# A list scheduler orders the first phase of a gated scan and feed-forward kernel; low parts and clips change engines

## The chip, the cores and the metric

The kernel runs on one core of one Trainium2 chip. The metric is device time in microseconds (us) of one execution. Engines are named as in the profile: PE is TensorE's matmul, PEld its weight load, DVE is VectorE, ACT is ScalarE, POOL is GpSimd, SP is SyncE, whose queue issues the DMA transfers here.

## The reference

Two parts follow each other. A gated recurrence over 6080 positions of 2 sequences with 256 channels, and a feed-forward layer on all 12160 tokens (256 to 2048 to 256), in float32:

```
sig = 1 / (1 + exp(-f_logit));  f = lb + (1 - lb) * sig;  i = 1 - f
h[t] = f[t] * h[t-1] + i[t] * x[t]            # per channel
a = h @ w_in                                  # 256 -> 2048
g = a where a >= 1;  0 where a <= -1;  (a + 1)**2 / 4 between
y = g @ w_out                                 # 2048 -> 256
```

The weights are float64 in memory: they arrive as pairs of 32-bit words and are turned into floats on the chip.

## The kernel before

**Tiles and numbers.** Channels lie on the 128 partitions (two halves k), tokens along the free dimension. The tokens are cut into tiles of 384, 512, 512, 512, and then 512 each. Every number that TensorE multiplies is split into a high part (a cast to fp32r) and a low part (value minus high part), and each product is three matmuls: high by high, low weight by high, high by low. A *unit* (t, u) is tile t by 256 of the 2048 hidden channels, with two halves j. For each j there are six matmuls into a PSUM bank (`mm_h`, L294 to L303; *H block* here), then the activation, then six matmuls that add to the tile's two output banks (`mm_o`, L347; *O block*). "H20" below is the two H blocks of unit (2, 0).

**The activation** of one half: `clip` to -1..1 from the PSUM bank (DVE, L310), (c/2 + 1/2)**2 (ACT, L313), maximum with the bank (`top`, DVE, L318), which frees the bank, the cast to the high part (ACT, L325), the subtraction for the low part (`g_lo`, POOL, L332).

**The weights.** There are 17 jobs (two of half size), each a load of 512 KB, whose words are taken apart: `conv1a` masks the exponent (DVE, L149), shifts it (ACT, L150) and masks the fraction (DVE, L151); `conv1b` joins fraction and lower word (DVE, L160) and scales (ACT, L163); `conv2` adds the sign (DVE, L172), multiplies (DVE, L179 or L184), casts the high part (ACT, L185) and subtracts the low part (POOL, L186).

**The recurrence** of one tile and half: `gate` (ACT, L228), `inp` (DVE, L250), `forget` (ACT, L241), `scan` (DVE, L267), high part (ACT, L274), low part (POOL, L279).

**The phases.** The *first phase* takes tiles 0 to 2 through all eight u (24 units in eight *rounds* of three, u from 0 to 7) while the weights are converted. Its PE order in the loop is H block, O block of two units earlier, H block, O block; six of eight PSUM banks hold the outputs of three tiles, so that two are left for H blocks. Tile 3 follows alone (the loop at L788), then pairs of tiles in a plan of fixed times. In all phases the order of an engine's instructions is the order in which the program emits them. In the first phase this order is written out by hand: rounds from u = 1 run in the loop of L493, with one step of a list `fill` (a half of a conversion, or a step of tile 3's recurrence) behind each clip:

```
for j in JA:
    mm_h(t, u, [j])
    if j == 0 and i > T0:
        g_lo(*units[i - 1], nc.gpsimd)
    clip(t, u, j)
    step = fill.pop(0) if fill else None
    ...
    top(t, u, j)
    if i > T0:
        mm_o(*units[i - LAG], [j])
```

Of the kernel before, what the change touches and what calls it, by code (L numbers as in the profile page):

```python
# [7 lines left out]
F32 = mybir.dt.float32  # L8
BF16 = mybir.dt.bfloat16
F32R = mybir.dt.float32r  # L10
I32 = mybir.dt.int32
# [10 lines left out]
def token_tiles(total):  # L22

    out, s = [], 0
    while s < total:
        n = SIZES[len(out)] if len(out) < len(SIZES) else NMAX
        assert s + n <= total
        out.append((s, n))
        s += n
    return out  # L30


@with_exitstack
def gated_scan_then_ffn_kernel(
# [58 lines left out]
    mol = const.tile([P, KD], F32, name="mol")  # L93
    half = const.tile([P, 1], F32, name="half")
# [47 lines left out]
    def conv1a(j):  # L142
        r = raw[j]
        hi = r[..., 1]
        ea = sp.tile([P, 2, *hi.shape[1:]], I32, tag="s", name="ea")
        e, a = ea[:, 0], ea[:, 1]
        exps[j], mants[j] = e, a

        nc.vector.tensor_single_scalar(out=flat(e), in_=flat2(hi), scalar=0x7FF00000, op=ALU.bitwise_and)  # L149
        nc.scalar.activation(out=flat(e), in_=flat(e), func=AF.Relu, bias=ebias, scale=8.0)  # L150
        nc.vector.tensor_single_scalar(out=flat(a), in_=flat2(hi), scalar=0x000FFFFF, op=ALU.bitwise_and)  # L151

    flat2 = flat3 = flat

    def conv1b(j):

        lo = raw[j][..., 0].bitcast(U32)
        v = sp.tile(list(lo.shape), F32, tag="s", name="v")
        vals[j] = v
        nc.vector.scalar_tensor_tensor(  # L160
            out=flat(v), in0=flat(lo), scalar=2.0**-32, in1=flat(mants.pop(j)), op0=ALU.mult, op1=ALU.add
        )
        nc.scalar.activation(out=flat(v), in_=flat(v), func=AF.Identity, bias=one, scale=2.0**-20)  # L163

    def conv1(j):
        conv1a(j)
        conv1b(j)

    def conv2(j, eng):
        e, v = exps.pop(j), vals.pop(j)  # L170
        _, hi, lo = jobs[j]
        nc.vector.scalar_tensor_tensor(  # L172
            out=flat(e), in0=flat(raw.pop(j)[..., 1]), scalar=-0x80000000, in1=flat(e),
            op0=ALU.bitwise_and, op1=ALU.bitwise_or,
        )
        if len(v.shape) == 4:

            for k in range(KD):
                nc.vector.scalar_tensor_tensor(  # L179
                    out=flat3(v[:, k]), in0=flat3(v[:, k]), scalar=oml[:, k : k + 1],  # L180
                    in1=flat3(e[:, k].bitcast(F32)), op0=ALU.mult, op1=ALU.mult,
                )
        else:
            nc.vector.tensor_tensor(out=flat(v), in0=flat(v), in1=flat(e.bitcast(F32)), op=ALU.mult)  # L184
        nc.scalar.copy(out=hi, in_=v)  # L185
        eng.tensor_tensor(out=lo, in0=v, in1=hi, op=ALU.subtract)  # L186
# [107 lines left out]
    def mm_h(t, u, js=JA):  # L294
        n = tiles[t][1]
        for j in js:
            ops = []
            for w, x in ((wi_hi, xhi), (wi_lo, xhi), (wi_hi, xlo)):
                ops += [(w[:, u, k, j], x[t, k][:, :n]) for k in range(KD)]
            for i, (a, b) in enumerate(ops):  # L300
                nc.tensor.matmul(  # L301
                    out=acc[t, u][j][:, :n], lhsT=a, rhs=b, start=(i == 0), stop=(i == len(ops) - 1)
                )  # L303

    def clip(t, u, j):
        n = tiles[t][1]
        if (t, u) not in gg:
            gg[t, u] = gp.tile([P, 2, NMAX], F32, tag="g", name="g")
        c = gg[t, u][:, j, :n]
        nc.vector.tensor_scalar(  # L310
            out=c, in0=acc[t, u][j][:, :n], scalar1=-1.0, scalar2=1.0, op0=ALU.max, op1=ALU.min
        )
        nc.scalar.activation(out=c, in_=c, func=AF.Square, bias=half, scale=0.5)  # L313

    def top(t, u, j):
        n = tiles[t][1]
        c = gg[t, u][:, j, :n]
        nc.vector.tensor_tensor(out=c, in0=c, in1=acc[t, u][j][:, :n], op=ALU.max)  # L318

    def g_hi(t, u, js=JA):  # L320
        n = tiles[t][1]
        if js[0] == 0:
# [4 lines left out]
    def g_lo(t, u, eng, js=JA):  # L327
        n = tiles[t][1]
        if js[0] == 0:
# [43 lines left out]
    with tc.manual_schedule():  # L373
# [8 lines left out]
        load_x(0, K0, (fv, fin, "f"))  # L382
        nc.sync.dma_start(out=lb, in_=lower_bound.rearrange("(k p) -> p k", p=P))
        load_w(0)
        load_x(0, K0, (xv, xin, "x"))
        load_x(0, K1)
        load_w(1)
        load_x(1, KA)
        load_w(2)
        load_x(2, KA)  # L390
        nc.vector.tensor_scalar(
            out=oml, in0=lb, scalar1=-1.0, scalar2=1.0, op0=ALU.mult, op1=ALU.add
        )
# [12 lines left out]
        gate(1, K0)
        forget(1, K0, nc.scalar, True)
        inp(0, K1)
        scan(0, 1)
        x_hi(0, K1)  # L410
        x_lo(0, K1, nc.gpsimd)
        conv1(1)
        conv2(1, nc.gpsimd)
        gate(1, K1)
        forget(1, K1, nc.scalar, True)
        inp(1, K0)
        scan(1, 0)
        x_hi(1, K0)
        x_lo(1, K0, nc.gpsimd)
        gate(2, KA)  # L420
        inp(1, K1)
        scan(1, 1)
        x_hi(1, K1)
        x_lo(1, K1, nc.gpsimd)
# [4 lines left out]
        units += [(t, u) for t in range(T0, NC) for u in range(NU)]  # L429

        for t in range(3):
            acc[t, 0] = [bank(), bank()]
        mm_h(0, 0)
        clip(0, 0, 0)
        mm_h(1, 0)
        conv1a(2)
        for k in (K0, K1):
            inp(2, k)
            forget(2, k, nc.scalar)
        for k in (K0, K1):  # L440
            scan(2, k.start)
            x_hi(2, k)
            x_lo(2, k, nc.gpsimd)
        clip(0, 0, 1)
        conv1b(2)
        mm_h(2, 0)
        conv2(2, nc.gpsimd)
        for j in JA:
            top(0, 0, j)
            g_hi(0, 0, [j])  # L450
            g_lo(0, 0, nc.gpsimd, [j])
        for j in JA:
            clip(1, 0, j)
        keep_warm(6, po[0, 0])
        load_w(3)
        load_w(4)
        conv1a(3)
        conv1b(3)
        for j in JA:
            top(1, 0, j)  # L460
            g_hi(1, 0, [j])
            g_lo(1, 0, nc.gpsimd, [j])
        mm_o(0, 0)
        conv2(3, nc.gpsimd)
        mm_o(1, 0)
        for j in JA:
            clip(2, 0, j)
        for j in JA:
            top(2, 0, j)
            g_hi(2, 0, [j])  # L470
            g_lo(2, 0, nc.gpsimd, [j])

        def late_steps(t):
            return [
                lambda: gate(t, KA),
                lambda: [inp(t, k) for k in (K0, K1)],
                lambda: [forget(t, k, nc.scalar) for k in (K0, K1)],
                lambda: scan(t, 0),
                lambda: scan(t, 1),
                lambda: [x_hi(t, k) for k in (K0, K1)],  # L480
                lambda: [x_lo(t, k, nc.gpsimd) for k in (K0, K1)],
            ]

        fill = []
        late = late_steps(T0)
        for u in range(1, NU):
            for j in (2 + 2 * u, 3 + 2 * u):
                if j < NJ:
                    fill += [lambda j=j: conv1(j), lambda j=j: conv2(j, nc.gpsimd)]
            fill += [late.pop(0) if late else None, late.pop(0) if late else None]  # L490

        nl = 5
        for i in range(3, n0):  # L493
            t, u = units[i]
            if i == T0:
                load_x(T0, KA)
            if i == 2 * T0:
                load_x(T0 + 1, KA)
            if i % T0 < 2 and nl < NJ:
                load_w(nl)  # L500
                nl += 1
            acc[t, u] = [bank(), bank()]
            for j in JA:
                mm_h(t, u, [j])
                if j == 0 and i > T0:
                    g_lo(*units[i - 1], nc.gpsimd)
                clip(t, u, j)
                step = fill.pop(0) if fill else None
                if step:
                    step()  # L510
                top(t, u, j)
                if i > T0:
                    mm_o(*units[i - LAG], [j])
            g_hi(t, u)
            if units[i - LAG][1] == NU - 1:
# [318 lines left out]
```

## Time and profile before

| | |
|---|---|
| median of 3 runs | 1059.85 us (1059.76 to 1060.99) |
| the profiled execution | 1061.0 us |
| its span, first to last instruction | 1059.2 us |
| mean granted TensorE clock | 0.987 of full speed |
| PE busy in the span | 96% |

Busy time is the time in which an engine had an instruction in it. Neighbouring instructions overlap by some hundredths of a microsecond, so that a row of them costs less than the sum of their durations; the distance from one start to the next is called *pitch* here.

### The profile page before, as it was taken

How to read it: one execution, taken by the hardware profiler on the slowest of the kernel's cores; microseconds unless marked ns; L12 is line 12 of the kernel's file. 1: busy time of each engine (PE TensorE's matmuls, PEld its weight loads, DVE VectorE, ACT ScalarE, POOL GpSimd, SP SyncE). 2: the span in 40 equal slices, each digit the busy share in tenths (PEclk: the TensorE clock that was granted, in tenths of full speed). 3: DMA queues.
4: the chain of work that ended last, by engine and by line, in shares of the span. 5: the costliest groups of instructions: out<-in, count | busy, mean ns of one | idle time of the engine just before them, and what ended most of it. 6: DMA issues, size and time to landing. Idle time of an engine off the chain costs nothing.

```text
span 1059.2 us, 12755 instructions
## 1 busy us (share of the span) xinstructions
PE 1014.5 (96%) x4414; PEld 827.8 (78%) x4414; DVE 766.9 (72%) x1112; ACT 704.1 (66%) x1130; POOL 716.6 (68%) x536
## 2 busy tenths in 40 slices
PE   6788889999989999999999999999999999999997
PEld 3566668788768888888888888888888888888886
DVE  7989885667767766766767767766776776766665
ACT  5556555656567667667668667667667768767564
POOL 2545544767787687687677777677677677777544
PEclk7999999999999999999999999999999999999999
DMA  7211101211002002002002002002002002000001
GB/s 248 81 59 60 46 15 55 80 51 50 1 1 100 20 1 100 20 0 100 20 1 100 21 1 100 21 1 100 20 1 98 22 1 69 12 1 31 11 1 40
DMA packets 26897, 46.56 MB, mean 44 GB/s; under 512 B 2256, under 2 KB 7120, under 8 KB 26832
## 3 DMA queue, kind: packets, MB, share of 16 engines
q1 hardware_dynamic: 26544, 45.23, 12.9%
q8 instruction: 34, 0.56, 0.2%
q10 hardware_dynamic: 288, 0.52, 0.1%
q14 instruction: 31, 0.25, 0.1%
HBM read 33.29 MB, written 12.45 MB: 43 GB/s over the span
## 4 chain that ended last, share of the span: by engine, by line
PE 72%; DVE 4%; ACT 4%; issue 1%; POOL 1%; DMA 0%; ACTq 0%; DVEq 0%; POOLq 0%
PE bank L343 39%; PE bank L568 32%; ACT g L617 1%; ACT ghi L624 1%; PE bank L301 1%; DVE g L199 1%; DVE g L621 1%; DVE g L203 1%; DVE g L610 1%; DVE h L267 0%; DVE g L204 0%; ACT s_hi L206 0%; POOL glo L332 0%; POOL x L250 0%; DMA out_dram<-o 0%
## 5 line engine op out<-in xcount | busy, mean ns | idle before, releaser
L627 POOL TENSOR_TENSOR glo<-g,ghi 128x512 fp32r<-128x512 f32 x320 | 415.6, 1310 | 216.7 <-ACT ghi L624 179.2
L621 DVE TENSOR_TENSOR g<-g,bank 128x512 f32<-128x512 f32 x320 | 219.4, 686 | 119.2 <-ACT g L617 119.2
L343 PE MATMUL bank<-glo,wo_hi 128*128 128x512 f32 (+1 forms) x768 | 299.9, 390 | 5.2 <-POOL glo L332 3.6
L343 PE MATMUL bank<-ghi,wo_hi 128*128 128x512 f32 (+1 forms) x768 | 299.1, 389 | 1.8 <-ACT ghi L325 1.3
L343 PE MATMUL bank<-ghi,wo_lo 128*128 128x512 f32 (+1 forms) x768 | 298.8, 389 | 0.0
L617 ACT ACTIVATE g<-g,half 128x512 f32<-128x512 f32 x320 | 225.7, 723 | 108.2 <-DVE g L610 107.0
L624 ACT CAST ghi<-g 128x512 fp32r<-128x512 f32 x320 | 192.0, 624 | 77.9 <-DVE g L621 69.7
L610 DVE TENSOR_SCALAR g<-bank 128x512 f32<-128x512 f32 x320 | 213.8, 687 | 1.0 <-PE bank L568 0.6
L343 PEld LDWEIGHTS bank<-glo,wo_hi 128*128 128x128 f32 x768 | 145.1, 189 | 37.9 <-POOL glo L332 5.7
L343 PEld LDWEIGHTS bank<-ghi,wo_hi 128*128 128x128 f32 x768 | 145.0, 189 | 31.5 <-ACT ghi L325 1.6
L343 PEld LDWEIGHTS bank<-ghi,wo_lo 128*128 128x128 f32 x768 | 145.2, 189 | 29.6 <-POOL wo_lo L186 0.3
L568 PE MATMUL bank<-xhi,s_hi 128*128 128x512 f32 x288 | 112.2, 390 | 1.7 <-ACT bank L590 1.7
L593 DVE TENSOR_TENSOR bank<-bank,snap 128x512 f32<-128x512 f32 x72 | 50.4, 700 | 86.4 <-ACT ghi L624 82.0
L568 PE MATMUL bank<-xhi,s_lo 128*128 128x512 f32 x288 | 112.1, 389 | 0.0
L568 PE MATMUL bank<-xlo,s_hi 128*128 128x512 f32 x288 | 112.0, 389 | 0.0
L568 PE MATMUL bank<-xhi,wi_hi 128*128 128x512 f32 x280 | 109.3, 390 | 1.2 <-DVE g L621 1.2
L568 PE MATMUL bank<-xlo,wi_hi 128*128 128x512 f32 x280 | 109.0, 389 | 0.0
L568 PE MATMUL bank<-xhi,wi_lo 128*128 128x512 f32 x280 | 108.9, 389 | 0.0
L332 POOL TENSOR_TENSOR glo<-g,ghi 128x1024 fp32r<-128x1024 f32 (+3 forms) x35 | 79.7, 2282 | 34.9 <-issue 28.4
L597 DVE TENSOR_TENSOR bank<-bank,snap 128x512 f32<-128x512 f32 x72 | 50.4, 699 | 32.4 <-PE bank L568 32.2
L301 PE MATMUL bank<-xhi,wi_hi 128*128 128x512 f32 (+1 forms) x128 | 43.6, 419 | 27.2 <-DVE g L318 17.0
L568 PEld LDWEIGHTS bank<-xhi,s_hi 128*128 128x128 f32 x288 | 54.0, 188 | 13.5 <-ACT bank L590 2.3
(64 smaller groups left out, 1254.2 us busy)
## 6 DMA issues: line engine op xcount, KB each, us to landing
f<-in_fT SPq DMA_DIRECT2D x23, 512.0 KB, 4.2
x<-in_xT SPq DMA_DIRECT2D x23, 512.0 KB, 4.7
out_dram<-o SPq DMA_DIRECT2D x44, 256.0 KB, 2.0
raw<-in_w_out SPq DMA_DIRECT2D x8, 512.0 KB, 3.6
raw<-in_w_in SPq DMA_DIRECT2D x14, 256.0 KB, 3.3
raw<-in_w_in SPq DMA_DIRECT2D x4, 128.0 KB, 3.2
out_dram<-o ACTq DMA_DIRECT2D x2, 256.0 KB, 2.0
f<-in_fT SPq DMA_DIRECT2D x2, 192.0 KB, 3.1
```

The costliest lines, as they stand in the source:

```text
L199: nc.vector.tensor_tensor(out=w[:, :4].rearrange("p a b -> p (a b)"), in0=flat(wi_hi[:, u]), in1=flat(wi_lo[:, u]), op=ALU.add)
L301: nc.tensor.matmul(out=acc[t, u][j][:, :n], lhsT=a, rhs=b, start=(i == 0), stop=(i == len(ops) - 1))
L332: eng.tensor_tensor(out=glo[t, u][:, s, :n], in0=gg[t, u][:, s, :n], in1=ghi[t, u][:, s, :n], op=ALU.subtract,)
L343: nc.tensor.matmul(out=po[t, d][:, :n], lhsT=w, rhs=r, start=(first and q == 0), stop=(last and q == 2))
L568: nc.tensor.matmul(out=dst, lhsT=w, rhs=r, start=(start and q == 0), stop=(q == 2), skip_group_check=True,)
L593: nc.vector.tensor_tensor(out=B[g, "Z"], in0=B[g, "Y"], in1=snaps[g], op=ALU.add)
L597: nc.vector.tensor_tensor(out=B[g, "V"], in0=B[g, "Y"], in1=snaps[g], op=ALU.add)
L610: nc.vector.tensor_scalar(out=gtile(gG, g, b, F32, "g"), in0=B[g, blocks[b][0]], scalar1=-1.0, scalar2=1.0, op0=ALU.max, op1=ALU.min,)
L617: nc.scalar.activation(out=c, in_=c, func=AF.Square, bias=half, scale=0.5)
L621: nc.vector.tensor_tensor(out=c, in0=c, in1=B[g, blocks[b][0]], op=ALU.max)
L624: nc.scalar.copy(out=gtile(hG, g, b, F32R, "ghi"), in_=gtile(gG, g, b, F32, "g"))
L627: nc.gpsimd.tensor_tensor(out=gtile(lG, g, b, F32R, "glo"), in0=gtile(gG, g, b, F32, "g"), in1=gtile(hG, g, b, F32R, "ghi"), op=ALU.subtract,)
```

## The change

The first phase is no longer written out. Each step becomes an entry in a `Plan` with an engine, a duration in us, and the steps that it has to follow. At build time a list scheduler gives each step a start: PE and SP keep their written order, DVE, ACT and POOL take what can start first (within 0.15 us, what is due first). Steps of DVE that touch SBUF alone ("DVE*") and all of POOL also wait for a common resource "port", so in the plan no two of them overlap. The steps are then emitted in order of planned start. Nothing in the program makes POOL and DVE exclude each other when it runs: the plan sets each engine's order alone.

```
+            for n in able:
+                e = ops[n][0]
+                if e in fixed and fixed[e][0] != n:
+                    continue
+                t = max(idle[e.strip("*")], ready[n])
+                if e in ("DVE*", "POOL"):
+                    t = max(t, idle["port"])
+                key = (t, latest(n))
...
+        start = self.times({n: due.get(n, t + 10.0) for n in self.ops})
+        for n in sorted(start, key=start.get):
+            f, args = self.ops[n][3:]
+            f(*args)
```

Steps change engine as well. The low parts of the recurrence and of the weights go from POOL to DVE; of the low parts of g, those of j = 1 go to DVE and those of j = 0 stay on POOL, each half by itself:

```
+        def add_low(name, z, after, on_dve, f, *args):
+            if on_dve:
+                add(name, "DVE*", 0.08 + 0.54 * z, after, f, *args, nc.vector)
+            else:
+                add(name, "POOL", 0.17 + 1.1 * z, after, f, *args, nc.gpsimd)
...
+                add_low(("xlo", t, k), z, [("xhi", t, k)], True, x_lo, t, s1)
...
+                    add_low((kind, j), z, deps, True, f)
...
+                add(("ghi", t, u, j), "ACT", 0.1 + 0.43 * z, deps, g_hi, t, u, [j])
+                add_low(("glo", t, u, j), z, [("ghi", t, u, j)], j == 1, g_lo, t, u, [j])
```

The clips of j = 1, and all of u = 0, go from DVE to ACT, as two Relu in place of one clip, and a square without scale:

```
+        nc.scalar.activation(out=c, in_=acc[t, u, j][:, :n], func=AF.Relu, bias=half, scale=-0.5)
+        nc.scalar.activation(out=c, in_=c, func=AF.Relu, bias=one, scale=-1.0)
...
+                if j == 1 or u == 0:
+                    add(("clip", t, u, j), "ACT", 0.2 + 0.9 * z, deps, clip_act, t, u, j)
+                else:
+                    add(("clip", t, u, j), "DVE", 0.06 + 0.55 * z, deps, clip, t, u, j)
```

In a conversion of w_in the factor `oml` goes from two multiplications on DVE into ACT's scaling (one instruction for each k), and the value is one DVE multiplication; the joined value takes the place of the fraction, with no buffer of its own. The PE order begins with

```
+        head = "H00 H10 O00 H01 O10 H11 O01 H20 O11 H21 O20 H02".split()
```

where it was H00 H10 H20 O00 O10, and goes on as before, O two units behind H. The six matmuls on zeros between (`keep_warm(6, ...)`) are gone. On SP the load of job 3 is issued before tile 2's, tile 3's and 4's come after those of jobs 8 and 10. In the tile-3 loop nothing is changed but names.

**DVE, a stretch of round u = 2**: two units' halves and the end of one conversion and the beginning of the next (L310 and L422 are the clip, L318 and L449 the maximum, L184 and L287 the value, L296 and L463 the low parts). Before:

```order
L184 TENSOR_TENSOR v_514<-v_514,ea_510 128x512
L318 TENSOR_TENSOR g_507<-g_507,bank_498 128x384
L310 TENSOR_SCALAR g_557<-bank_547 128x512
L149 TENSOR_SCALAR ea_560<-raw_494 128x512
L151 TENSOR_SCALAR ea_560<-raw_494 128x512
L160 SCALAR_TENSOR_TENSOR v_564<-raw_494,ea_560 128x512
L318 TENSOR_TENSOR g_557<-g_557,bank_547 128x512
L310 TENSOR_SCALAR g_557<-bank_548 128x512
L172 SCALAR_TENSOR_TENSOR ea_560<-raw_494,ea_560 128x512
```

The changed kernel:

```order
L287 TENSOR_TENSOR ea_459<-ea_459 128x512
L449 TENSOR_TENSOR g_528<-g_528,bank_530 128x384
L422 TENSOR_SCALAR g_567<-bank_544 128x512
L244 TENSOR_SCALAR ea_570<-raw_272 128x512
L254 TENSOR_SCALAR ea_570<-raw_272 128x512
L449 TENSOR_TENSOR g_567<-g_567,bank_544 128x512
L296 TENSOR_TENSOR wo_lo_91<-ea_459,wo_hi_90 128x512
L262 SCALAR_TENSOR_TENSOR ea_570<-raw_272,ea_570 128x512
L280 SCALAR_TENSOR_TENSOR ea_570<-raw_272,ea_570 128x512
L463 TENSOR_TENSOR glo_565<-g_528,ghi_555 128x384
L449 TENSOR_TENSOR g_567<-g_567,bank_575 128x512
```

The second half's clip is gone from DVE, the low parts of the weight and of g's second half have come.

**POOL, the same round.** Before:

```order
L186 TENSOR_TENSOR wo_lo_90<-v_514,wo_hi_89 128x512
L332 TENSOR_TENSOR glo_555<-g_507,ghi_543 128x2x384
L186 TENSOR_TENSOR wi_lo_88<-v_564,wi_hi_87 128x512
L332 TENSOR_TENSOR glo_604<-g_557,ghi_594 128x1024
L332 TENSOR_TENSOR glo_648<-g_606,ghi_635 128x1024
```

The changed kernel:

```order
L463 TENSOR_TENSOR glo_565<-g_528,ghi_555 128x384
L463 TENSOR_TENSOR glo_609<-g_567,ghi_586 128x512
L463 TENSOR_TENSOR glo_669<-g_623,ghi_665 128x512
```

What is left on POOL is the low part of one half per unit.

**ACT, one unit of 512 columns in that round** (L435 and L436 are the two Relu, L444 the square behind DVE's clip, L442 the one behind ACT's, L456 the cast of g, L251, L272 and L292 steps of a conversion). The changed kernel:

```order
L444 ACTIVATE g_567<-g_567,half_83 128x512
L251 ACTIVATE ea_570<-ea_570,ebias_85 128x512
L456 CAST ghi_586<-g_567 128x512
L435 ACTIVATE g_567<-bank_575,half_83 128x512
L436 ACTIVATE g_567<-g_567,one_84 128x512
L442 ACTIVATE g_567<-g_567 128x512
L272 ACTIVATE ea_570<-ea_570,oml_80,omls_82 128x256 x2
L456 CAST ghi_586<-g_567 128x512
```

Before, the same unit had two squares (L313), the conversion's steps, and one cast of 1024.

## Rows read from the trace of the kernel before

**Rows 1.** The page's first part: busy us, share of the span and instructions of each engine.

```profile
span 1059.2 us, 12755 instructions
PE 1014.5 (96%) x4414; PEld 827.8 (78%) x4414; DVE 766.9 (72%) x1112; ACT 704.1 (66%) x1130; POOL 716.6 (68%) x536
```

**Rows 2.** Busy time of each engine by stage: startup, rounds u = 1 to 6, round u = 7, all that follows.

```profile
core 0: us, PE busy (x) PEld busy (x) DVE busy (x) ACT busy (x) POOL busy (x), PEclk, DMA share, GB/s
9.50:43.10 33.60, 22.78 (x67) 15.03 (x68) 31.12 (x38) 18.81 (x32) 17.75 (x14) 0.75 0.53 183
43.10:157.90 114.80, 97.04 (x422) 78.11 (x420) 102.47 (x142) 65.88 (x95) 59.79 (x33) 0.97 0.15 46
157.90:173.60 15.70, 15.53 (x74) 13.17 (x74) 11.62 (x18) 8.60 (x13) 9.38 (x5) 1.00 0.00 1
173.60:1059.20 885.60, 873.66 (x3841) 719.52 (x3840) 617.52 (x902) 605.14 (x982) 628.92 (x481) 1.00 0.11 37
```

**Rows 3.** PE's timeline (start us, busy us, line, operands, count, idle before and what ended it): the first H block, the first block of H01, an O and an H block of 384 columns at the start of round u = 7 (156.83, 157.89), the H and O blocks of 512 columns behind one another (162.79, 164.16), and the first block of tile 3, where the first phase ends.

```profile
9.52 0.44 PE L301 MATMUL bank<-xhi,wi_hi 128*128 128x384 f32 x1 [2.67 <-ACT wi_hi L185]
...
43.08 0.51 PE L301 MATMUL bank<-xhi,wi_hi 128*128 128x384 f32 x2
...
156.83 0.33 PE L343 MATMUL bank<-ghi,wo_hi 128*128 128x384 f32 x1
...
157.89 0.54 PE L301 MATMUL bank<-xhi,wi_hi 128*128 128x384 f32 x2
...
162.79 0.62 PE L301 MATMUL bank<-xhi,wi_hi 128*128 128x512 f32 x2
...
164.16 0.39 PE L343 MATMUL bank<-ghi,wo_hi 128*128 128x512 f32 x1
...
173.59 0.63 PE L301 MATMUL bank<-xhi,wi_hi 128*128 128x512 f32 x2
```

**Rows 4.** Who waited for whom in rounds u = 1 to 6, 43 to 158 us (us in total, times, longest): all of PE's waits there, and the longest two of ACT and of DVE.

```profile
PE bank L301 <- DVE g L318: 16.8, 12, 2.1
PE bank L343 <- DVE g L318: 0.5, 1, 0.5
...
ACT v L163 <- DVE v L160: 14.8, 8, 2.5
ACT g L313 <- DVE g L310: 10.4, 13, 2.0
...
DVE g L318 <- ACT g L313: 8.3, 8, 1.2
DVE g L310 <- PE bank L301: 1.9, 3, 1.0
```

**Rows 5.** Groups of instructions by line and shape, 0 to 160 us (busy us, mean ns of one, idle before): DVE's clip and maximum, three steps of the conversions, and POOL's three low parts.

```profile
L310 DVE TENSOR_SCALAR g<-bank 128x512 f32<-128x512 f32 x28 | 19.0, 684 | 0.9 <-PE bank L301 0.9
L318 DVE TENSOR_TENSOR g<-g,bank 128x512 f32<-128x512 f32 x28 | 18.9, 681 | 9.3 <-ACT g L313 9.3
L151 DVE TENSOR_SCALAR ea<-raw 128x512 int32<-128x512 int32 x14 | 18.7, 1337 | 0.0
L172 DVE SCALAR_TENSOR_TENSOR ea<-raw,ea 128x512 int32<-128x512 int32 x14 | 15.7, 1124 | 0.0
L149 DVE TENSOR_SCALAR ea<-raw 128x512 int32<-128x512 int32 x14 | 13.4, 959 | 0.0
L186 POOL TENSOR_TENSOR wo_lo<-v,wo_hi 128x512 fp32r<-128x512 f32 x7 | 9.1, 1296 | 18.9 <-ACT wo_hi L185 18.9
L332 POOL TENSOR_TENSOR glo<-g,ghi 128x1024 fp32r<-128x1024 f32 x11 | 28.8, 2617 | 10.2 <-issue 10.2
L332 POOL TENSOR_TENSOR glo<-g,ghi 128x384 fp32r<-128x384 f32 x2 | 2.2, 1102 | 0.0
```

**Rows 6.** Timeline of DVE and POOL: two low parts on POOL, with a clip and a sign step of DVE begun under them; then a mask and a sign step with POOL idle.

```profile
26.45 3.19 POOL L279 TENSOR_TENSOR xlo<-h,xhi 128x512 fp32r<-128x512 f32 x2 [3.42 <-ACT xhi L274]
26.81 0.53 DVE L310 TENSOR_SCALAR g<-bank 128x384 f32<-128x384 f32 x1
28.43 1.75 DVE L172 SCALAR_TENSOR_TENSOR ea<-raw,ea 128x512 int32<-128x512 int32 x1
...
126.91 0.68 DVE L172 SCALAR_TENSOR_TENSOR ea<-raw,ea 128x512 int32<-128x512 int32 x1
...
141.78 0.42 DVE L149 TENSOR_SCALAR ea<-raw 128x512 int32<-128x512 int32 x1
142.11 0.42 DVE L151 TENSOR_SCALAR ea<-raw 128x512 int32<-128x512 int32 x1
```

**Rows 7.** DVE's timeline, for pitches: a scan pair, 384 columns, 512 columns.

```profile
24.43 2.46 DVE L267 TENSOR_TENSOR_SCAN h<-f,h,x 128x512 f32<-128x512 f32 x2 [0.26 <-ACT f L241]
...
107.69 0.55 DVE L318 TENSOR_TENSOR g<-g,bank 128x384 f32<-128x384 f32 x1
108.15 0.68 DVE L310 TENSOR_SCALAR g<-bank 128x512 f32<-128x512 f32 x1
...
112.09 0.69 DVE L160 SCALAR_TENSOR_TENSOR v<-raw,ea 128x512 f32<-128x512 uint32 x1
112.70 0.68 DVE L318 TENSOR_TENSOR g<-g,bank 128x512 f32<-128x512 f32 x1
113.30 0.68 DVE L310 TENSOR_SCALAR g<-bank 128x512 f32<-128x512 f32 x1
```

**Rows 8.** ACT, for pitches: its timeline (a cast of 512 followed by one of 768; a square of 384 and two activations of 512 behind one another), and the line of a later phase in which ACT reads a PSUM bank (ns min/median/max).

```profile
107.80 0.62 ACT L185 CAST wo_hi<-v 128x512 fp32r<-128x512 f32 x1 [1.99 <-DVE v L184]
108.33 0.83 ACT L325 CAST ghi<-g 128x768 fp32r<-128x768 f32 x1
...
142.45 0.61 ACT L313 ACTIVATE g<-g,half 128x384 f32<-128x384 f32 x1
142.97 0.70 ACT L150 ACTIVATE ea<-ea,ebias 128x512 int32<-128x512 int32 x1
143.58 0.71 ACT L163 ACTIVATE v<-v,one 128x512 f32<-128x512 f32 x1
...
L585 ACT COPY snap<-bank x72: 578/593/597, 317.0 to 1040.0; 128x512 f32<-128x512 f32 x72
```

**Rows 9.** The first weight on DVE and the first gate of tile 1 on ACT, each released by a DMA transfer.

```profile
4.88 0.29 DVE L149 TENSOR_SCALAR ea<-raw 128x256 int32<-128x256 int32 x1 [1.20 <-DMA raw<-in_w_in]
...
11.43 0.63 ACT L228 ACTIVATE f<-f 128x512 f32<-128x512 f32 x1 [1.97 <-DMA f<-in_fT]
```

More of the change, by code (lines that the diff above doesn't have):

```diff
@@ L153, in gated_scan_then_ffn_kernel @@
[L153 to L186, printed above, removed]
@@ L484, in gated_scan_then_ffn_kernel @@
[L484 to L502, printed above, removed]
-            for j in JA:
[L504 to L515, printed above, removed]
-                for d in range(KD):
-                    finish(units[i - LAG][0], d)
@@ new lines, in load, with add_load_x @@
+        def load(name, mb, after, f, *args):
+            add(("load", *name), "SP", mb / 0.26, after, f, *args)
+        def add_load_x(t, k, which):
+            after = []
+            if which[2] == "f" and t >= 3:
+                after = [("scan", t - 3, k) for k in range(KD)]
+            if which[2] == "x" and t >= 2:
+                after = [("scan", t - 2, k) for k in range(KD)]
+            kk = range(KD) if k is None else [k]
+            load(
+                (which[2], t, k), 0.25 * len(kk) * size(t), after, load_x, t,
+                slice(kk[0], kk[-1] + 1), which,
+            )
@@ new lines, in add_load_w @@
+        def add_load_w(j):
+            load(("w", j), 0.25 if j < 2 else 0.5, [("sign", j - 4)] if j > 3 else [], load_w, j)
+        XF = ((fv, fin, "f"), (xv, xin, "x"))
+        add_load_x(0, 0, XF[0])
+        load(("lb",), 0.1, [], lambda: nc.sync.dma_start(out=lb, in_=lower_bound.rearrange("(k p) -> p k", p=P)))
+        add_load_w(0)
+        add_load_x(0, 0, XF[1])
+        for w in XF:
+            add_load_x(0, 1, w)
+        add_load_w(1)
+        for w in XF:
+            add_load_x(1, None, w)
@@ new lines, in gated_scan_then_ffn_kernel @@
+        for j in range(NJ):
+            z = 0.5 if j < 2 else 1.0
+            kinds = "exponent", "rebias", "fraction", "join", "mantissa", "sign", "value", "high", "low"
+            eng = "DVE*", "ACT", "DVE*", "DVE*", "ACT", "DVE*", "DVE*", "ACT", "POOL"
+            dur = 0.36, 0.65, 0.36, 0.62, 0.75, 0.62, 0.62, 0.53, 1.27
+            start = [("load", "w", j)] + ([("low", j - 3)] if j > 2 else [])
+            before = {
+                "rebias": ["exponent"], "fraction": ["exponent"], "join": ["fraction"], "mantissa": ["join"],
+                "sign": ["rebias"], "value": ["sign", "mantissa"], "high": ["value"], "low": ["high"],
+            }
+            for kind, e, d, f in zip(kinds, eng, dur, split_steps(j)):
+                deps = [(b, j) for b in before.get(kind, [])] or start
+                if kind == "mantissa":
+                    deps.append(("const",))
+                if kind == "low":
+                    add_low((kind, j), z, deps, True, f)
+                else:
+                    add((kind, j), e, 0.1 + (d - 0.1) * z, deps, f)
@@ new lines, in gated_scan_then_ffn_kernel @@
+        head = "H00 H10 O00 H01 O10 H11 O01 H20 O11 H21 O20 H02".split()
+        first = [(x[0], int(x[1]), int(x[2])) for x in head]
+        done = {x[1:] for x in first if x[0] == "H"}
+        rest = [x for x in units[:n0] if x not in done]
+        pe = [(k, t, u, j) for k, t, u in first for j in JA]
+        order = [x[1:] for x in first if x[0] == "H"] + rest
+        oorder = [x[1:] for x in first if x[0] == "O"]
+        for t, u in rest:
+            o = [x for x in order if x not in oorder][0]
+            oorder.append(o)
+            for j in JA:
+                pe.append(("H", t, u, j))
+                pe.append(("O", *o, j))
@@ L793, in gated_scan_then_ffn_kernel @@
                 clip(t, u, j)
-                if j == 0:
-                    g_lo(*units[i - 1], nc.gpsimd)
+                square(t, u, j)
+                if j == 0 and i > n0:
+                    g_lo(*units[i - 1], JA, nc.gpsimd)
                 steps.pop(0)()
```

330 lines of the change are left out of this document (216 added, 114 removed).

## The prediction

> **What bounds the kernel now.** I read the page's busy shares first, then the busy time by stage, then PE's timeline and waits in the first phase, and last single instructions of DVE and POOL. The page says PE, 96% busy [rows 1], so only a stage in which PE stands still has something to give. By stage that is the first phase alone: it ends at 173.6 us, where tile 3's first block starts [rows 3], and behind it PE is busy for 873.7 of 885.6 us [rows 2]. The change touches nothing behind that point but names, so its whole effect is how far that point moves.
>
> PE's work up to there is fixed. A block of six matmuls of 512 columns takes 1.37 us (162.79 to 164.16), one of 384 about 1.07 (156.83 to 157.89 to 158.9) [rows 3]. The phase holds H blocks of 24 units and O blocks of 22 (the last two come later): 32 blocks of 384 and 60 of 512, 34.2 + 82.2 = 116.4 us. It lasts from 9.5 to 173.6, 164.1 us. A round of three units is 8 x 1.37 + 4 x 1.07 = 15.2 us of PE work. Rounds u = 1 to 6 took 114.8 us, 19.1 each; round u = 7, in which one weight job is converted and not two, took 15.7 [rows 2]. So what costs PE 3.4 us a round goes with the conversions.
>
> In rounds 1 to 6 PE waits 17.3 us, all for the maximum on DVE, which frees the H bank [rows 4]; it also runs there at a mean clock of 0.97 and in the startup at 0.75 [rows 2]. DVE is busy 102.5 of 114.8 us [rows 2], but much of that is standing: the mask L149 and L151 take 0.42 us with POOL idle and the sign step L172 0.68 [rows 6], while their means over the phase are 0.96, 1.34 and 1.12 [rows 5]. The reason stands in one place: a sign step begun at 28.43 under POOL's low parts (until 29.64) ends at 30.18, 0.54 after them, though a clip from PSUM begun under the same low part takes its normal 0.53 [rows 6]. Clips and maxima of 512 columns have means of 0.68 over all their executions [rows 5]: they aren't held. These three lines alone lose 14 x (0.54 + 0.92 + 0.44) = 27 us, with clip and maximum queued behind them.
>
> **The change, part by part.** I take DVE's pitches as 0.61 for 512 columns, 0.47 for 384, 0.33 for a mask, 1.18 for a scan [rows 6, 7], and 0.68 for a sign step; ACT's as 0.61 for an activation, 0.53 for a cast, 0.52 and 0.42 at 384 columns [rows 8].
>
> *DVE.* Out: 27 of 48 clips, about 15 us. In: 16 weights' worth of low parts (9.8), eight low parts of the recurrence (4.6) and 24 of g (13.5). The product with oml costs nothing new: one multiplication of 0.61 stands for two halves. What DVE now has in the phase: conversions 15 x 3.18 + 2 x 1.9 = 51.5; recurrence of four tiles 18.1; 21 clips 11.8; 48 maxima 27.0; low parts 13.5. Together 121.9 us.
>
> *POOL.* Left are 24 low parts of one half, 1.29 us each (1.10 at 384) [rows 5]: 3.6 us a round in place of about 10 (59.8 over six rounds [rows 2]).
>
> *ACT.* The two Relu are not in the trace. Bounds for the pair: from below two casts, 2 x 0.53; from above two activations at full duration, 1.4. I take 1.21: the reading of a bank took 0.59 us without a bias [rows 8], an activation 0.61. 27 pairs are 31.0 us. All of ACT: conversions 30.8, recurrence 13.4, pairs 31.0, squares 27.8, casts of g by halves 23.7, two output copies 1.0, together 127.7 us; a round is 14.2 us, where ACT was busy 65.9 / 6 = 11.0 [rows 2]. The two ends of the pair change a round by -0.4 and +0.6 us.
>
> *PE's new head* lets PE work on tiles 0 and 1 while tile 2 is still being made: before H20 stand 8 blocks of 384 and 6 of 512, 16.8 us, where 12.5 us were done at 43.1 in the old order. When can H20 start? ACT can't pass tile 1's gate before its transfer lands at 11.43 [rows 9], and from there to tile 2's high parts the order gives it 27.8 us: 39.2. DVE starts at 4.88 [rows 9] and has 32.3 us up to tile 2's low parts: 37.2. Waits between the two come on top; I add 3 us, about the three low parts that POOL has before H20, and take **42**, between 39 and 46.
>
> *Edits with no price:* the six matmuls on zeros ran where PE waited (clock 0.75 in the startup [rows 2]; at that clock 16.8 us would be 22, still inside 32). The loads move on SP, but in rounds 1 to 6 no wait of PE is for a transfer [rows 4] and the DMA engines are busy 15% [rows 2]; if that cover went, a late load would add its delay once. The tile-3 loop starts from the same state. Plan durations only set the order.
>
> *The sum.* From H20 PE has 116.4 - 16.8 = 99.6 us to the end of the phase. DVE then has 89.6 and ACT about 95, so PE is the longest by little. How much is lost on it? Round 7 shows 15.7 for 15.2 with ACT 8.6 and DVE 11.6 us busy [rows 2]; rounds 1 to 6 show 19.1. The new rounds lie nearer the first, since DVE is no longer held for long; but with ACT at 14.2 and DVE at 13.8 us some banks will come late, and I add 0.4 us, half of the mean wait that DVE had for a square (8.3 us in 8 [rows 4]): 16.1 us, a factor of 1.06. The phase ends at 42 + 99.6 x 1.06 = 147.5 instead of 173.6: 26.1 us less. The profiled execution was 1061.0, so 1034.9; the median of the runs lies 1.15 lower, at 1059.85, which makes **1033.7 us**. With the start between 39 and 46 and rounds of 15.6 to 16.7 us this case reaches from 1029 to 1040.
>
> **The rivals.** *Cleaner:* H20 at 39 and all rounds like round 7 (1.033): the phase ends at 141.9, time 1028. For it: PE, DVE and ACT all have the room on paper. Against: ACT at 93% of PE's pace in order.
>
> *The holds stay.* Nothing makes POOL and DVE exclude each other on the chip; only the orders are set. If each of POOL's 21 low parts after H20 meets a DVE step from SBUF and holds it to the end, DVE has 89.6 + 27.1 us and is the bound: 42 + 116.7 = 158.7, 14.9 us less, 1045. For it: DVE's steps from SBUF are two thirds of its time. Against: 39 us of DVE's work are clips and maxima that are not held [rows 5], and the hold has to be full each time. The Trainium skill, "SBUF — State Buffer", in the section on who interferes with whom, speaks for this rival: issue order decides who blocks, and who comes first keeps the shared pair for its whole instruction. The trace agrees in the held sign step [rows 6].
>
> *The change doesn't do what it says:* the holds are not what sets PE's pace, and the freed DVE time turns into waits for ACT. From 43.1 the old order took 130.5 us for 103.9 of PE's work, a factor of 1.26. With that, 42 + 125.1 = 167.1, 6.5 us less, 1053: only the new head pays. Against: round 7.
>
> *Slower: the H bank comes back too late from ACT.* There are two H banks; a bank's way was clip 0.68, square 0.72, maximum 0.68, and for j = 1 becomes Relu, Relu, square, maximum, about 2.7 us, in an ACT queue with weights' casts between. PE gives it 4.1 us (O, H, O). If the queues add over 1.4 us each time, PE waits at every H block. There are 34 after the head, so the gain of 32 us that a phase without any wait would have (141.6) is gone at 32 / 34 = 0.94 us per block; at 1.15 the phase ends at 180.7, time 1067. Against: in the old rounds the mean was 16.8 / 36 = 0.47 with DVE held [rows 4]; it would have to double.
>
> **How the numbers follow.** Forecast 0.50, cleaner 0.19, holds stay 0.15, only the head pays 0.09, slower 0.04, and 0.03 that effects cancel to within 0.2%, 1057.7 to 1062, about what a measurement of this kernel can tell. The range of 1025 to 1046 takes in the first three cases with their spread and leaves out 0.16. Faster by over 0.2%: 0.93; same 0.03; slower 0.04.
>
> **What would show it.** Tile 3's first block at about 147 us (142 to 155). H20 at 42 or so. Rounds of 16 us, with PE's waits under 1 us a round, where they were 2.9. DVE's masks and sign step near 0.42 and 0.68 us, with POOL under 4 us busy in a round. DVE and ACT both busy for some 85 to 90% of a round. All behind the first phase takes 885.6 us as before. It is wrong if H20 comes after 46, if the masks still have means near 1 us, or if PE waits for the maximum or for squares by 2 us and more in a round.

## The result and the profile after

The changed kernel takes 1031.76 us (median of 4 runs, 1031.03 to 1033.05) against 1060.42 (4 runs of the kernel before on the same chip): a ratio of 0.9731, 95% interval 0.9714 to 0.9748. The forecast was 1033.7. The profiled execution took 1032.4 us with a span of 1030.6, 28.6 less than before.

All of it came from the first phase. PE's timeline of the changed kernel, at the places of [rows 3]: the first H block, the first of H20, the start of round u = 3, and tile 3's first block (L414 is the H block's matmul).

```profile
13.57 0.69 PE L414 MATMUL bank<-xhi,wi_hi 128*128 128x384 f32 x1 [6.14 <-ACT wi_hi L292]
...
42.18 1.05 PE L414 MATMUL bank<-xhi,wi_hi 128*128 128x512 f32 x2
...
68.58 0.44 PE L414 MATMUL bank<-xhi,wi_hi 128*128 128x384 f32 x1
...
144.90 0.39 PE L414 MATMUL bank<-xhi,wi_hi 128*128 128x512 f32 x1
```

Tile 3 starts at 144.90 and not at 173.59, 28.7 us earlier: the whole difference of the spans. By stage, as in [rows 2] (startup to H20; from there to round u = 3; rounds u = 3 to 6; round u = 7; all that follows):

```profile
9.50:42.18 32.68, 23.25 (x84) 18.35 (x85) 30.60 (x53) 30.03 (x56) 3.36 (x3) 0.77 0.71 241
42.18:68.58 26.40, 24.91 (x110) 20.25 (x109) 22.84 (x39) 24.56 (x44) 6.19 (x5) 0.97 0.17 54
68.58:129.72 61.14, 61.14 (x288) 52.81 (x289) 58.01 (x97) 56.83 (x100) 15.34 (x12) 1.00 0.11 35
129.72:144.90 15.18, 15.18 (x74) 13.21 (x74) 13.94 (x23) 14.24 (x25) 3.31 (x3) 1.00 0.00 0
144.90:1030.60 885.70, 873.91 (x3841) 719.48 (x3840) 620.63 (x906) 605.37 (x984) 627.78 (x481) 1.00 0.11 37
```

From 68.58 on PE is busy without a gap, 61.14 of 61.14 us and 15.18 of 15.18: five rounds in 76.3 us, 15.3 each, where rounds took 19.1. The granted clock is full there, 1.00 for 0.97. 15.3 us is the length of PE's own work, 15.2. DVE and ACT are busy 92 to 95% beside it and PE waits for neither. Behind the first phase nothing changed, 885.70 us for 885.60. The waits of that stretch, all that DVE and ACT have between 68.58 and 129.72, are short, and none of PE's matmuls waits (two of its weight loads do, 0.5 us in all):

```profile
ACT ghi L456 <- DVE g L449: 1.9, 5, 0.5
DVE glo L463 <- ACT ghi L456: 1.4, 4, 0.5
ACT g L435 <- PE bank L414: 1.1, 4, 0.4
DVE g L422 <- PE bank L414: 0.8, 2, 0.5
ACT g L444 <- DVE g L422: 0.4, 1, 0.4
...
DVE g L449 <- ACT g L442: 0.2, 1, 0.2
```

The masks and the sign step are hardly held any more. The same groups as in [rows 5], 0 to 160 us of the changed kernel (L244 and L254 are the masks L149 and L151, L280 the sign step L172), and two of the low parts that came to DVE:

```profile
L280 DVE SCALAR_TENSOR_TENSOR ea<-raw,ea 128x512 int32<-128x512 int32 x15 | 11.3, 756 | 0.0
L254 DVE TENSOR_SCALAR ea<-raw 128x512 int32<-128x512 int32 x15 | 6.4, 427 | 0.0
L244 DVE TENSOR_SCALAR ea<-raw 128x512 int32<-128x512 int32 x15 | 6.3, 420 | 0.0
L463 POOL TENSOR_TENSOR glo<-g,ghi 128x512 fp32r<-128x512 f32 x16 | 22.1, 1384 | 73.3 <-ACT ghi L456 50.2 <-PE bank L474 11.8 <-issue 11.3
...
L463 DVE TENSOR_TENSOR glo<-g,ghi 128x384 fp32r<-128x384 f32 x8 | 7.7, 960 | 0.0
...
L296 DVE TENSOR_TENSOR wi_lo<-ea,wi_hi 128x512 fp32r<-128x512 f32 x7 | 5.9, 840 | 0.3 <-ACT wi_hi L292 0.3
```

The masks have means of 0.42 and 0.43 us in place of 0.96 and 1.34; of 27 us in three groups 1 us is left. The moved low parts are held instead: 0.96 us on average for 384 columns, which take 0.54 when free, and 0.84 for the weights' 512, which take 0.68. One hold of about 1.1 us comes in each of the rounds u = 3 to 6, three of the four on a low part of g, as here, where the step on DVE begins under POOL's and ends 0.41 us after it:

```profile
93.77 1.52 POOL L463 TENSOR_TENSOR glo<-g,ghi 128x512 fp32r<-128x512 f32 x1 [2.39 <-issue]
```

```profile
94.05 1.65 DVE L463 TENSOR_TENSOR glo<-g,ghi 128x384 fp32r<-128x384 f32 x1
```

DVE had time for it: PE waits for nothing in these rounds.

### The profile page after: what moved, and what is told of

Same layout as the page of the kernel before. It is cut to its first block, busy times and chain, and to the rows that moved or that the text cites. A ratio compares the mean times of both kernels' runs of the same rounds, so it can differ in the third digit from the quotient of the medians.

```text
span 1030.6 us, 12789 instructions
## 1 busy us (share of the span) xinstructions
PE 1004.5 (97%) x4408; PEld 826.2 (80%) x4408; DVE 750.4 (73%) x1126; ACT 736.6 (71%) x1216; POOL 656.7 (64%) x508
## 4 chain that ended last, share of the span: by engine, by line
PE 74%; DVE 4%; ACT 3%; issue 1%; POOL 1%; DMA 0%; ACTq 0%; DVEq 0%; POOLq 0%
PE bank L474 40%; PE bank L725 33%; ACT g L774 1%; PE bank L414 1%; ACT ghi L781 1%; DVE g L311 1%; DVE g L315 1%; DVE g L778 1%; DVE g L767 1%; DMA out_dram<-o 0%; ACT s_hi L318 0%; DVE h L379 0%; DVE g L316 0%; POOL glo L784 0%; POOL glo L463 0%
## 5 line engine op out<-in xcount | busy, mean ns | idle before, releaser
L463 POOL TENSOR_TENSOR glo<-g,ghi 128x512 fp32r<-128x512 f32 (+2 forms) x32 | 51.9, 1622 | 129.2 <-ACT ghi L456 88.9
L747 ACT COPY bank<-bank 128x512 f32<-128x512 f32 x72 | 41.2, 572 | 34.0 <-PE bank L725 34.0
```

Source lines behind the costliest of these rows:

```text
L463: eng.tensor_tensor(out=glo[t, u][:, s, :n], in0=gg[t, u][:, s, :n], in1=ghi[t, u][:, s, :n], op=ALU.subtract,)
L747: nc.scalar.copy(out=B[g, "Q"], in_=B[g, "Y"])
```

## The experiments

The change has three parts: an order by a list scheduler, a rule in it that keeps POOL and DVE's SBUF steps apart, and steps that change engine. The runs first cross them. Medians in us; the kernel before ran beside each of them:

| order | old engines | new engines |
|---|---|---|
| written by hand | 1060.4 to 1060.8 (before) | 1093.3 |
| scheduler, no port rule | 1060.0 | 1039.9 |
| scheduler with port rule | 1051.2 | 1031.8 (the change) |

The columns aren't pure. The scheduler's rows also hold the rest of the change, of which only the new head was run by itself: the product with oml on ACT, the casts of g by halves, the moved loads, no matmuls on zeros. The row written by hand has the old form of all these.

The traces of the same six runs say how long DVE was held. The next table adds up, until tile 3's first block, what DVE's steps from SBUF took beyond the usual time of their shape (0.41 us for a mask, 0.68 for 512 columns, 0.54 for 384), where that is over 0.1 us:

| DVE held, us (steps) | old engines | new engines |
|---|---|---|
| written by hand | 36.2 (35) | 7.6 (17) |
| scheduler, no port rule | 38.8 (49) | 10.5 (15) |
| scheduler with port rule | 23.3 (35) | 9.1 (14) |

Most of the held time goes with the new engines, in every order, and yet the slowest run is among them. So the holds alone don't set the time.

**plan_old_engines.** The changed kernel with

```
-                add_low(("xlo", t, k), z, [("xhi", t, k)], True, x_lo, t, s1)
+                add_low(("xlo", t, k), z, [("xhi", t, k)], False, x_lo, t, s1)
...
-                    add_low((kind, j), z, deps, True, f)
+                    add_low((kind, j), z, deps, False, f)
...
-                if j == 1 or u == 0:
+                if False:
                     add(("clip", t, u, j), "ACT", 0.2 + 0.9 * z, deps, clip_act, t, u, j)
...
-                add_low(("glo", t, u, j), z, [("ghi", t, u, j)], j == 1, g_lo, t, u, [j])
+                add_low(("glo", t, u, j), z, [("ghi", t, u, j)], False, g_lo, t, u, [j])
```

> The list scheduler with its port rule, but every step on its old engine (all low parts on POOL, each half of g by itself, all clips on DVE). Theory 1, holds: POOL's low parts (48 of g, 59 us by 1.29 and 1.10; 31 us of weights and recurrence) and DVE's steps from SBUF (55 us) cannot overlap, 145 us in a row from about 5 us, with waits some 155 to 160 for the first phase: 1041 to 1047 us. Rival, the order alone pays: as the changed kernel, 1031 to 1035. Rival, the move of engines alone pays: as before, 1055 to 1060.

Measured 1051.18 us, ratio 0.9908 (0.9893 to 0.9923): neither rival, and 4 us beyond the theory's range. The phase ended at 160.45 us, as late as foreseen or a little later. Most of the rest lies behind it, where the kernel took 889.0 us in place of 885.7: tile 3's first block still waited 2.1 us for a low part on POOL, and after PE had stood for 2.1 us before 160.45 its granted clock was 0.51 on average up to 170. The estimated 145 us of steps that exclude each other were a floor here, with waits on top; they did not all keep apart either, DVE was still held for 23.3 us.

**plan_no_port** and **plan_old_engines_no_port.** The changed kernel, and the one above, with

```
-                if e in ("DVE*", "POOL"):
+                if False:
                     t = max(t, idle["port"])
...
-                    if ops[m][0] in ("DVE*", "POOL"):
+                    if False:
                         tm = max(tm, idle["port"])
```

> The changed kernel with the port rule taken out of the scheduler; engines as in the change. Theory 1, holds: POOL's 24 low parts meet DVE steps from SBUF about two times in three and hold them for half their length on average, 24 x 0.67 x 0.65 = 10 us on a DVE that is busy 13.9 of 15.2 us in a round: 3 to 8 us slower than the change, 1035 to 1040, and the masks and sign steps of DVE above their 0.42 and 0.68 us. Rival, the move of engines is all: within 1 us of the change, 1031 to 1033.

> Neither port rule nor moved steps: only a list scheduler's order in place of the hand-written one, and the new head. Theory 1, holds: DVE has 108 us of its own and up to 30 us of holds: 1043 to 1055, slower than the same with the port rule. Rival, the order alone pays: 1031 to 1035.

Measured 1039.87 us, ratio 0.9798 (0.9781 to 0.9815; the profiled execution, 1036.9, was its fastest), and 1060.02, ratio 0.9992 (0.9982 to 1.0001). So the rule is worth 8.1 us with the new engines and 8.8 with the old ones, in time as the theory had it for the first. The second came out worse than expected: a scheduler's order with old engines and without the rule gives nothing at all. In it the holds are as in the kernel before: mask 1.04, second mask 0.95, sign step 1.10 us on average, and the rule takes 15.5 us of held time away. With the new engines the trace does not bear the theory out: DVE is held for 10.5 us without the rule and 9.1 with it, with the first mask (0.63 us on average) and the low parts of w_out (0.87) held longer than in the change and those of g less. The rule also changes which step comes when, so where these 8.1 us come from is not shown; the profile is of the fastest run and has 4.5 of them. The timelines of POOL and of DVE in plan_no_port show one of its holds, a low part of a weight of DVE (L296) begun under POOL's low part of 96.84 to 98.13:

```profile
96.84 1.29 POOL L463 TENSOR_TENSOR glo<-g,ghi 128x512 fp32r<-128x512 f32 x1 [4.64 <-PE bank L414]
```

```profile
96.87 0.69 DVE L422 TENSOR_SCALAR g<-bank 128x512 f32<-128x512 f32 x1
97.48 1.20 DVE L296 TENSOR_TENSOR wo_lo<-ea,wo_hi 128x512 fp32r<-128x512 f32 x1
98.60 0.68 DVE L463 TENSOR_TENSOR glo<-g,ghi 128x512 fp32r<-128x512 f32 x1
```

The clip at 96.87 reads PSUM and takes its normal 0.69; the subtraction behind it takes 1.20 where the next one takes 0.68, and ends half a microsecond after POOL.

**pool_double.** The changed kernel with one more subtraction on POOL ahead of each of its low parts in the first phase:

```
+        if spare and eng is nc.gpsimd:
+            for _ in range(1):
+                eng.tensor_tensor(out=spare[0][:, :n], in0=spare[0][:, :n], in1=spare[0][:, :n], op=ALU.subtract)
...
+        spare.append(op.tile([P, NMAX], F32, tag="snap", name="spare", bufs=1))
+        nc.gpsimd.memset(spare[0], 0.0)
         plan.run()
+        spare.clear()
```

> The changed kernel with one more subtraction of the same size on POOL ahead of each of its 24 low parts, on a spare tile that nothing reads; the plan does not know of them. Theory 1, holds: 28 us of POOL work that the plan did not keep apart from DVE's steps from SBUF; two thirds of it meets such a step and holds it for half its length or more, 10 to 18 us on DVE, of which some 1.2 us a round are taken up by its idle time: 1034 to 1046, with DVE's steps from SBUF clearly longer. Rival, no holds that matter: POOL was idle for over 11 us of each round, so within 1 us of the change, 1031 to 1033.

Measured 1037.43 us, ratio 0.9786 (0.9771 to 0.9801): 5.7 us more than the change, from work that nobody waits for on an engine that was idle three quarters of the time. The order of the other steps is the change's, so this run is the plainest test of the holds. PE's share of the stretch that had no gap shows it, and the second mask and the sign step (0 to 145 us) are held again:

```profile
68.58:129.72 61.14, 58.62 (x269) 48.56 (x269) 58.45 (x91) 53.05 (x93) 27.71 (x23) 1.00 0.12 36
```

```profile
L280 DVE SCALAR_TENSOR_TENSOR ea<-raw,ea 128x512 int32<-128x512 int32 x15 | 13.9, 927 | 0.0
...
L254 DVE TENSOR_SCALAR ea<-raw 128x512 int32<-128x512 int32 x15 | 11.1, 740 | 0.0
```

DVE is held for 19.8 us in 30 steps, 10.7 us more than in the change, and tile 3 starts at 150.26, 5.4 us later. POOL's own low parts come later too, but up to there PE never waits for one of them: its waits are for DVE and ACT.

**plan_clips_dve** and **plan_clips_act.** The condition `j == 1 or u == 0` for ACT's clips becomes `False` or `True`.

> The changed kernel with all clips on DVE. DVE gets 15 us more, 137 us in all, 15.5 us in a round against PE's 15.2, and ACT 31 us less. Theory, DVE would be the bound: rounds of 16 to 17.5 us and 6 to 14 us more than the change, 1038 to 1046. Rival, ACT at 14.2 us a round is what limits: no slower than the change, 1029 to 1033.

> The changed kernel with all clips on ACT: 21 pairs of Relu more, 25 us, and 12 us less on DVE. ACT then has 153 us in the phase, 17.6 us in a round. Theory, engines in balance: ACT is the bound, the phase ends near 165, 1049 to 1054. Rival, DVE's time is what limits: no slower than the change, 1029 to 1033.

Measured 1046.37 (ratio 0.9867, 0.9853 to 0.9882) and 1052.10 (0.9928, 0.9912 to 0.9945), both as the theory of balanced engines had it, the first 0.4 us beyond the end of its range. With all clips on ACT, that engine has no room left. Its busy times from 60 to 140 us:

```profile
60.00:140.00 80.00, 72.94 (x326) 58.24 (x324) 57.50 (x92) 78.58 (x140) 15.43 (x13) 1.00 0.12 38
```

ACT is busy 78.58 of 80 us and PE 72.94. With all clips on DVE it is DVE, 74.98 of 80:

```profile
60.00:140.00 80.00, 74.45 (x333) 59.16 (x331) 74.98 (x126) 52.71 (x88) 18.00 (x14) 1.00 0.11 34
```

In both, part of the loss falls at the end of the phase: tile 3's recurrence is what the scheduler puts off, and tile 3's first block then waits for its high part, 3.61 us with all clips on ACT and 4.30 with all on DVE:

```profile
159.91 0.72 PE L414 MATMUL bank<-xhi,wi_hi 128*128 128x512 f32 x2 [4.30 <-ACT xhi L386]
```

**plan_clips_only** (all low parts back on POOL, clips as in the change) and **plan_glo_pool** (both low parts of g on POOL, `j == 1` becoming `False` in `add_low`).

> The changed kernel with all low parts back on POOL; the clips stay moved to ACT, the port rule stays. Theory, the shared resource: POOL's 89 us and DVE's 55 us of SBUF steps in a row are 145 us whatever the clips do, so the moved clips give little: 1045 to 1051, where the same with old clips took 1051.2. Rival, the moves add up: the clips give the 14.6 us that they give beside moved low parts (1046.4 to 1031.8), 1035 to 1038.

> The changed kernel with both low parts of g on POOL; those of the weights and of the recurrence stay on DVE. Port in the plan: DVE 121.9 - 13.5 - 38.8 (clips, maxima) = 69.6 us, POOL 58.9, together 128.5 us where the change has 112. Theory, the shared resource: over the 130 us that PE needs with the startup, so some us lost: 1034 to 1042. Rival, any relief of DVE helps: 1028 to 1032.

Measured 1041.36 (ratio 0.9814, 0.98 to 0.9829), between the two expectations, and 1037.49 (0.9781, 0.9765 to 0.9798), as the shared resource had it. The clips by themselves give 9.8 us (1051.2 to 1041.4), the low parts by themselves 4.8 (1051.2 to 1046.4), and together 19.4: more than the sum. Each alone leaves something full: with clips on DVE it is DVE (above); with low parts on POOL the masks and the sign step are held again, 0.76, 0.76 and 0.99 us on average.

**plan_old_head.** PE's order begins as in the kernel before:

```
-        head = "H00 H10 O00 H01 O10 H11 O01 H20 O11 H21 O20 H02".split()
+        head = "H00 H10 H20 O00 O10 H01 O20 H11 O01 H21 O11 H02".split()
```

> The changed kernel with H20 third in PE's order as before (H00 H10 H20 O00 O10 H01 O20 ...), the rest planned the same way. Theory: PE waits for tile 2 at about 37 us with 9.6 us of work ahead of it in place of 16.8, and DVE and ACT make tile 2 earlier at the cost of the first O blocks: 3 to 7 us more, 1035 to 1039. Rival, startup is bound by DVE and ACT whatever PE's order: within 1 us of the change.

Measured 1031.18 us, ratio 0.9728 (0.9713 to 0.9742): the rival. H20 starts at 25.78 us there and tile 3 at 144.77, where the change has 42.18 and 144.90. ACT was busy 30.0 of the startup's 32.7 us in the change, DVE 30.6: what PE does first makes no difference here.

**hand_lows_dve.** The kernel before with `nc.vector` in place of `nc.gpsimd` in all calls of `conv2` and `x_lo` of the first phase.

> The kernel before in its written order, with the low parts of the recurrence and of the weights moved to DVE and nothing else. Theory 1, holds: POOL loses 31 us of the steps that hold, DVE gains 14 us of work; the masks and sign steps are still held by g's low parts of two halves (2.6 us each): a small gain or none, 1050 to 1060. Rival, the move of engines is all: most of the gain, 1034 to 1042.

Measured 1073.83 us, ratio 1.0124 (1.0108 to 1.0139), slower by 13 us, which neither side had. The second mask is down to 0.55 us on average there (0 to 190 us), but DVE waits for ACT's casts, 9.3 us in 13 waits from 43 to 172 us. **hand_new_engines** then moves the rest in the written order:

```
+        if t < T0 and (j == 1 or u == 0):
+            nc.scalar.activation(out=c, in_=acc[t, u][j][:, :n], func=AF.Relu, bias=half, scale=-0.5)
+            nc.scalar.activation(out=c, in_=c, func=AF.Relu, bias=one, scale=-1.0)
+            nc.scalar.activation(out=c, in_=c, func=AF.Square)
+            return
...
-                    g_lo(*units[i - 1], nc.gpsimd)
+                    g_lo(*units[i - 1], nc.gpsimd, [0])
+                    g_lo(*units[i - 1], nc.vector, [1])
```

> The hand-written order with the change's engines: low parts of weights and recurrence on DVE, those of g split between POOL and DVE, clips of j = 1 and u = 0 on ACT. Theory, the order is needed for the moves: DVE now waits in its queue for ACT's casts, as in the run with the low parts alone (1073.8), 1050 to 1070. Rival, the moves pay by themselves, as they do under the scheduler without port rule (1060.0 to 1039.9): 1038 to 1045.

Measured 1093.31 us, ratio 1.0308 (1.0293 to 1.0323): 33 us slower than before, with the engines of the change, which is 29 us faster than before. The holds are mostly gone there too (second mask and sign step 0.42 and 0.68 us on average; the first mask is still held, 0.76). DVE's waits for ACT's casts from 43 to 190 us say what came in their place:

```profile
DVE glo L337 <- ACT ghi L330: 19.7, 19, 1.3
...
DVE wi_lo L186 <- ACT wi_hi L185: 7.3, 7, 1.1
DVE wo_lo L186 <- ACT wo_hi L185: 6.7, 6, 1.1
```

A low part needs ACT's cast of the same value. On POOL, in the written order, it waited at nobody's cost (44.3 us in 12 waits for casts of weights, 43 to 158 us, with no matmul of PE waiting for POOL); on DVE it stands right behind the step that feeds the cast, and the next maximum, and so the bank, stands behind it: 33.7 us in 32 waits. One of them, value, low part and maximum of DVE in that run:

```profile
101.99 0.69 DVE L184 TENSOR_TENSOR v<-v,ea 128x512 f32<-128x512 f32 x1
103.80 0.69 DVE L186 TENSOR_TENSOR wo_lo<-v,wo_hi 128x512 fp32r<-128x512 f32 x1 [1.11 <-ACT wo_hi L185]
104.40 0.55 DVE L323 TENSOR_TENSOR g<-g,bank 128x384 f32<-128x384 f32 x1
```

**hand_new_engines_late** emits these low parts half a unit later:

```
+        low = lambda: eng.tensor_tensor(out=lo, in0=v, in1=hi, op=ALU.subtract)
+        if later is None:
+            low()
+        else:
+            later.append(low)
...
+                for low in later:
+                    low()
+                later.clear()
+                if j == 1 and i > T0:
+                    g_lo(*units[i - 1], nc.vector, [1])
                 step = fill.pop(0) if fill else None
```

> The hand-written order with the change's engines (1093.3 us), with DVE's low parts emitted half a unit later: those of the weights behind the next clip, those of g's j = 1 behind the next unit's second clip, so that ACT's cast is done when DVE comes to them. Theory, what the moves cost in the written order is DVE's waiting in its queue for ACT's casts, 33.7 us from 43 to 190 us: most of it goes, 1060 to 1070. Rival, the rest of the written order is what the moves don't fit: 1085 to 1094.

Measured 1057.94 us, ratio 0.9976 (0.9966 to 0.9987): 35 us less than without, a little more than the 30.7 us of waits for casts that went (3.0 are left), and 2 us better than the theory's range. PE's waits for the maximum fall to a quarter (43 to 190 us; hand_new_engines, then this run):

```profile
PE bank L301 <- DVE g L323: 34.8, 29, 2.7
```

```profile
PE bank L307 <- DVE g L329: 8.3, 15, 1.4
```

What is left to the scheduler's 1039.9 with the same engines, 18 us, was not taken apart further.

## Why the prediction was right, and where it was not

*The place.* Right: the whole gain lies before tile 3's first block, and the 885.6 us behind it stayed.

*The start of H20.* Forecast 42, measured 42.18. The reason was half wrong. The limit is the work of ACT and DVE in the startup, as the sum of their orders said: tile 2's high parts were done at 41.2 and its low parts at 41.9. That 42 came out to 0.2 us is in part luck, since 3 us of it were an allowance for waits. That PE's new head gains anything by filling the time is refuted by plan_old_head, where tile 2 is ready at 25.78 and the phase ends at the same time. So the rival in which "only the new head pays", 6.5 us, had no such mechanism behind it; with order and head alone the gain is 0.8 us, in an interval that takes in none (plan_old_engines_no_port).

*The rounds.* Forecast 16.1 us, measured 15.3. This is the one term of the sum mis-sized: from u = 3 on the 0.4 us that I added to round 7's 15.7 for late banks did not come, and neither did that round's own half microsecond. The loss that I had spread over all rounds stands before u = 3: from H20 to there PE has 99.6 - 5 x 15.2 = 23.6 us of work and took 26.4. There it waits for a bank 1.5 us in two waits, all that it has from 42 to 145 us, and runs at a mean clock of 0.97. In all it took 102.7 us for 99.6, a factor of 1.03 and not 1.06. The phase then ended 2.6 us earlier than forecast (144.9 for 147.5), and the median lies 1.9 us lower.

*The engine sums.* DVE 13.8 us a round forecast, 14.5 measured over four rounds (58.01 / 4), of which 1.2 are holds; ACT 14.2 and 14.2 (56.83 / 4); POOL 3.6 and 3.8. At these shares PE loses nothing, but there is little room left: some 15 us more on DVE cost 14.6 and some 25 us more on ACT 20.3 in the two clip runs.

*The holds.* The reading of the trace was right, and two pairs of runs show what holds cost: with POOL's work doubled DVE is held 10.7 us longer and 5.7 us are lost; with the rule on the old engines it is held 15.5 us less and 8.8 are gained. Without the rule on the new engines 8.1 us are lost, but hardly by more held time. The rival "the holds stay" was priced at 27.1 us of holds and 11 us over the forecast; 9.1 us are there, one of 1.1 us in each round from u = 3 to 6, and DVE's idle time took them up. The forecast did not say whether the rule is needed for it, only that orders are set. What took most of the held time away is the move of the steps: it is down to 7.6 us in the hand-written order with the new engines too.

*What the prediction had not seen* is that moving work and ordering it can't be priced apart. I costed the moved low parts at their durations, on the ground that DVE has room. In the written order the same moves, with those of the clips, cost 33 us, and DVE's low parts queueing behind ACT's casts are the cause: emitted later they cost nothing.

*The slower rival* needed 0.94 us of wait at each H block. Its place is real, as plan_clips_act shows with ACT busy 98% of the time, but even there the kernel stayed faster than before.

## What to carry to other kernels

Before moving a step to another engine, ask which instruction its new queue will stand behind while it waits for its input: a step that waited at no cost on an idle engine can stop the engine that frees the buffers. Where two engines hold each other up, count their exclusive steps as one engine with one sum, put that sum beside the other engines', and place the steps against each other; in this kernel DVE and ACT could be busy 92 to 95% of PE's time without a gap on PE, in an order that a build-time scheduler made from durations. Such a sum is a bound and not a forecast: the chip does not keep the planned times, and in every run with the rule some steps that the plan had kept apart met.

## What the runs showed of the hardware

A square without bias and scale is cheaper than one with a bias tile. ACT's groups in the changed kernel, 0 to 160 us:

```profile
L444 ACT ACTIVATE g<-g,half 128x512 f32<-128x512 f32 x18 | 13.0, 720 | 2.8 <-DVE g L422 2.7
L435 ACT ACTIVATE g<-bank,half 128x512 f32<-128x512 f32 x18 | 12.2, 679 | 2.3 <-PE bank L414 1.4 <-POOL glo L463 0.9
L442 ACT ACTIVATE g<-g 128x512 f32<-128x512 f32 x18 | 11.3, 630 | 0.4
```

L444 has the tile half as bias and takes 0.72 us, L442 has none and takes 0.63; read from PSUM with the bias (L435) it is 0.68. So ACT's clip of two Relu was paid back in part by the square behind it, which I had costed alike. The Trainium skill, "ScalarE: Activation LUTs", in the section "What ACT_TABLE_LOAD costs", gives about 93 ns for each pointer operand of an activation; the 90 ns here agree.

The hold works both ways: POOL's low part of 512 columns has a mean of 1.38 us in the changed kernel where it is 1.29 when nothing is in its way; the one of 93.77 above, begun under a sign step of DVE (93.45 to 94.14), took 1.52. And 24 subtractions that nobody waits for, on an engine with three quarters of its time free, cost the kernel 5.7 us. DVE's steps with an operand in PSUM are not held: in none of the 14 profiles, before and after among them, did one of them take over 0.02 us more than its shape's usual 0.68 or 0.54 us (0 to 150 us), while steps from SBUF took up to 2.2 us more (a mask of the kernel before, 2.62 us at 122.72).
